# The decays' transfer issued by ScalarE, a planner constant for late transfers, and GpSimd's zeros ordered behind VectorE's clamp

## Chip, core and metric

The kernel runs on one core of one Trainium2 chip. The metric is the device time of one execution in microseconds; lower is better.

## What is computed

A linear attention with a decaying state, followed by a two-layer network with an exact GELU. All inputs are float32.

```python
batch, n_heads, seq, head_dim = (4, 8, 768, 48)
for t in range(S):
    kt, vt, rt = (k[:, :, t], v[:, :, t], r[:, :, t])
    cur = np.einsum('bhd,bhe->bhde', u[None] * kt, vt)
    y[:, :, t] = np.einsum('bhd,bhde->bhe', rt, state + cur)
    state = w[None, :, :, None] * state + np.einsum('bhd,bhe->bhde', kt, vt)
# x: y transposed to (3072 tokens, 384)
h = x @ w_in                                   # 384 -> 2048
g = 0.5 * h * (1.0 + erf(h * inv_sqrt2))
return g @ w_out                               # 2048 -> 384
```

`w` holds the decays (one for each head and channel), `u` the bonus of the current step.

## The kernel before

The sequence is cut into 6 chunks of 128 steps (`NCH`), the heads into 4 pairs (`NP`). Within a chunk the attention is done with matrix products. The powers of the decays scale r and k. The products of scaled k and r give the scores, and a mask and a diagonal are put in. The scores times v, plus the old state times r, give y. A group is one pair of heads in one chunk. The groups of the first chunk (`first_group`) have no old state and are the prologue: for each, VectorE multiplies r and k of the current step into `RK` (L559) and scales them by the powers into `Ts` (L553). TensorE sums `RK` times `u` (`sum_pairs`, L567), and ScalarE copies the sums to `cs` (L572). ScalarE or GpSimd puts the sums on the diagonal of `Am` (L580, L514). TensorE makes the scores (L586), VectorE copies them past the mask (L591), and TensorE multiplies by v (`new`, L605; `gaps`, L599, spreads the fourth pair over rows that are free). `keep` splits y into a high and a low part (`x3` and `xx`, L527 and L528), which are the network's input.

The network runs in float32 precision with three products of float32r parts (high and low weights `wh` and `wl`, high and low input). It has 16 steps of 128 hidden units for each chunk, 96 in all: `moe1` (L848, nine matmuls of 128x512 into the bank `Hp`), two GELUs on ScalarE (L880, L881), a subtraction on VectorE (L882) and `moe2` (L892, nine matmuls into `O`). During the first 16 steps the weights come in through three buffers `raw` (`w_load`, L482). They are taken apart by ScalarE (L497 into `wa`, L500 into `wb`, L506 into `wh`) and VectorE (L502, L509). The buffers `wa` must be zero beforehand (L439), as must be one half of `E` be ones (L466).

The decays and the bonus are one small tensor, `wu_sb` (112 partitions of 48 bytes). `clamp` (L418 to L421) sets ones in `W` and writes the clamped decays there. `powers` (L427, six multiplications) and `inverses` (L433, L434) make all powers from it, and ScalarE's `state_powers` (L446, L448) and three copies to `E` (L469) read them.

The order of the work is not the order of the program text. Each piece is handed to a `Plan` with an engine, a cost in nanoseconds, a due time and the names it reads and writes. `play` simulates the engines and picks, on each engine, the ready piece with the earliest due time. `run` repeats this for `ROUNDS` rounds and then tries `SEARCH` random changes of due times, drawn from `SEED`. It keeps what lowers `cost`, which is the end of TensorE's work in the plan plus the same end with every transfer `LATE` (600 ns) later. The best order is then issued. On the chip each engine takes its instructions strictly in that order and waits on semaphores where data demand it. Where TensorE has a hole in the plan during the prologue, `play` puts in `heat`, a matmul on zeros (L408).

For a transfer the plan keeps a common bus: it begins 1,050 ns after its issue, moves 412 bytes per ns, and lands 1,550 ns (600 for small ones) after its last byte. One more term is for transfers that were queued for over 1,200 ns:

```python
end = bus + (self.DMA_FIXED if ns > 20000 else self.DMA_SMALL)
end += self.DMA_SPREAD * (queued > self.DMA_QUEUED and bus > self.DMA_LATE)
```

`bus` is the time at which the transfer's last byte moves, `DMA_SPREAD` is 1,300 and `DMA_LATE` 16,000. All loads are issued by SyncE (SP), in the order of the plan. The first is `wu_sb` (L373), and then come the four tiles `T` of the prologue (L364), `N` (L367, L369) and the weights (L482). GpSimd's memsets have no semaphore on VectorE's work: the plan alone places `E` and the second `wa` after the clamp (they read the name `P0`, which the clamp writes), and on the chip they start as soon as GpSimd comes to them.

Of the kernel before, what the change touches and what calls it, by code (L numbers as in the profile page):

```python
# [18 lines left out]
ALU = mybir.AluOpType  # L19
# [12 lines left out]
HALF = 64  # L32
# [3 lines left out]
WMIN, WMAX = 0.7, 1.25  # L36
# [9 lines left out]
VISITS = (1, 6, 11)  # L46
POOL_DUE, POOL_CLASH, POOL_PE = 8000, 550, 2000
SWAP_DUE = 50000
ROUNDS, SEARCH, SEED, SPAN, LATE = 12, 2500, 5, (5000, 108000), 600
ROUND = "a"  # L50
LOADS = (1, 2, 3, "w0", "w1", 4, "u", "w2", 5)
AT_LOADS, AT_E = 14000, 15000
# [6 lines left out]
class Plan:  # L59
# [5 lines left out]
    OWN = {"act": 110, "dve": 110, "pool": 90}  # L65
    LAG = {"pe": 220, "act": 140, "dve": 115, "pool": 90, "sp": 0, "do": 0}
    DMA_GAP, DMA_LEAD, DMA_FIXED, DMA_SMALL, DMA_LANES = 480, 1050, 1550, 600, 8
    DMA_RATE, DMA_QUEUED, DMA_SPREAD, DMA_LATE = 412.0, 1200, 1300, 16000

    def __init__(self, after):  # L70
        self.after = after
# [3 lines left out]
    def add(self, eng, ns, at, fn, r=(), w=(), port=None):  # L75
        n = len(self.ops)
        deps = set()
        for x in r:
            deps.add(self.writer.get(x))
            self.readers.setdefault(x, []).append(n)  # L80
        for x in w:
            deps.add(self.writer.get(x))
            deps.update(self.readers.pop(x, ()))
            self.writer[x] = n
        deps -= {None, n}
        self.ops.append((eng, ns, at, fn, deps, eng == "pool" if port is None else port))
        self.reads.append(set(r))
        self.writes.append(set(w))
        return n

    def dma(self, nbytes, at, fn, r=(), w=(), gap=None):
        self.gaps[self.add("sp", nbytes, at, fn, r, w)] = gap or self.DMA_GAP
# [186 lines left out]
def rwkv_gelu_mlp(tc, rkT, rkv, wuT, uN, wmlp, r, k, vT, w, u, out):  # L279
    nc = tc.nc  # L280
    with ExitStack() as ctx:
# [7 lines left out]
        def sb(shape, dt, name, pool=None):  # L289
            return (pool or wk).tile(shape, dt, name=name)  # L290
# [8 lines left out]
        wu_sb = sb([LP, 3 * NP], F32, "wu_sb", cst)  # L299
        w_sb = wu_sb[:, 0:NP]  # L300
# [9 lines left out]
        W = sb([LP, NP, KEYS + C], F32, "W", pro)  # L310
        WKs = W[:, :, KEYS:]
        back = sb([LP, NP, 1], F32, "back", pro)
        E = sb([LP, NP, 2, 2, HALF], F32, "E")
# [16 lines left out]
        wa = [wa_all[:, i] for i in range(2)]  # L330
# [14 lines left out]
        def after(ins, one, reason="row tiles"):  # L345
            tc.add_manual_dep(ins.ins, one.ins.name, mybir.DependencyInfo(
                mybir.DependencyClass.Sync, mybir.DependencyReason.DATA), reason=reason)

        plan = Plan(after)
        add, dma = plan.add, plan.dma  # L350
        dve = lambda n: 65 + n / 0.96
        dve2 = lambda n: 65 + n / 1.92
        act = lambda n: 60 + n / 1.2
        pool = lambda n: 200 + n * 2.1
# [7 lines left out]
        def load_group(gi, at, r=()):  # L362
            s = slot(gi)
            dma(C * 4096, at, lambda: nc.sync.dma_start(T[s], rkT[gi]), r=[x for x in r if x[:8] != "free raw"], w=[f"T{s}"])  # L364
            if gi == 0:
                for i, x in ((1, "v"), (0, "k")):
                    dma(C * 1536, AT_LOADS + 800 * gi, lambda i=i: nc.sync.dma_start(N[s][:, i], rkv[gi, :, 1 + i]), r=r, w=[f"N{x}{s}"])  # L367
            elif gi < NP:
                dma(C * 3072, AT_LOADS + 800 * gi, lambda: nc.sync.dma_start(N[s], rkv[gi, :, 1:]), r=r, w=[f"Nk{s}", f"Nv{s}"])  # L369
            else:  # L370
                dma(C * 4608, at + 1, lambda: nc.sync.dma_start(N[s], rkv[gi]), r=[x for x in r if x != "free wb"], w=[f"Nr{s}", f"Nk{s}", f"Nv{s}"])

        dma(5000, -10 ** 6, lambda: nc.sync.dma_start(wu_sb, wuT), w=["w_sb"])  # L373
        load_group(0, LATER)


# [11 lines left out]
        for dst, src, x in ((diag2, diag, "diag"), (past2, past, "past")):  # L388
            for h in range(2):
                add("act", 245, LATER, lambda dst=dst, src=src, h=h: nc.scalar.copy(  # L390
                    out=dst[64 * h:64 * h + 64], in_=src[64 * h:64 * h + 64, 64 - 64 * h:128 - 64 * h]),
                    r=[x], w=[f"{x}2{h}"])
# [22 lines left out]
        plan.heat_from = add("pe", 430 * HEATS, 10, warm_up, r=["zeros"], w=["H", "A0", "A1", "O0", "O1", "O2", "Y", "U"])  # L415


        def clamp():  # L418
            nc.vector.memset(W[:, :, HALF:HALF + 1], 1.0)
            nc.vector.tensor_scalar(out=W[:, :, HALF + 1:HALF + 2], in0=w_sb.unsqueeze(2), scalar1=WMIN, scalar2=WMAX,  # L420
                                    op0=ALU.max, op1=ALU.min)  # L421

        def powers():
            n = 1
# [7 lines left out]
        def inverses():  # L432
            nc.vector.reciprocal(out=back, in_=W[:, :, C:C + 1])  # L433
            return nc.vector.tensor_tensor(out=W[:, :, 0:HALF], in0=W[:, :, HALF:C], in1=back.to_broadcast([LP, NP, HALF]),  # L434
                                           op=ALU.mult)

        add("dve", 170, -10 ** 6, clamp, r=["w_sb"], w=["P0"], port=True)
        for n, x in enumerate(wa):
            add("pool", 750, 5, lambda x=x: nc.gpsimd.memset(x, 0), r=["P0"] * n, w=["wa"], port=False)  # L439
        add("dve", 1380, 5, powers, r=["P0"], w=["P"], port=True)  # L440
        add("dve", 560, 6, inverses, r=["P"], w=["Wi"], port=True)

# [20 lines left out]
        add("act", 400, LATER, flipped(WN), r=["O0"], w=["WN"])  # L463


        add("pool", 520, 5, lambda: nc.gpsimd.memset(E[32:64, :, :, 1], 1.0), r=["P0"], w=["E0"], port=False)  # L466
        for i, (src, dst, h) in enumerate(((slice(0, LP), slice(0, LP), 0), (slice(0, D), slice(64, LP), 1),
                                           (slice(64, LP), slice(0, D), 1))):
            add("act", 630, AT_E, lambda src=src, dst=dst, h=h: nc.scalar.copy(  # L469
                out=E[dst].rearrange("l p a h i -> l (p a) h i")[:, :, h],  # L470
                in_=W[src].rearrange("l p (a i) -> l (p a) i", a=2)[:, :, 32:32 + HALF]),
                r=["Wi", "P", "WKs"], w=[f"E{(1, 2, 0)[i]}"], port=False)
        EVERY = [f"E{i}" for i in range(3)]
        for h in range(2):
            add("act", 480, LATER, lambda h=h: nc.scalar.copy(
                out=WN2[64 * h:64 * h + 64], in_=WN[0:64, :, ::1 - 2 * h]), r=["WN"], w=[f"WN2{h}"], port=False)
# [692 lines left out]
```

## Time and profile before

| | |
|---|---|
| median of 3 runs | 448.24 us (448.08 to 448.69) |
| profiled execution, its own time | 448.02 us |
| its span, first to last instruction | 446.3 us |
| mean granted TensorE clock | 0.998 |
| first 128x512 matmul of the network | 24.38 us after the span's start |
| last matmul ends | 441.8 us |

The span is what the rows below are counted in. The profiled execution took 1.72 us more than its span and 0.22 us less than the median of the runs. In the page and the rows PE is TensorE's matmuls, PEld its weight loads, DVE VectorE, ACT ScalarE, POOL GpSimd and SP SyncE. A q behind a name is the engine's sequencer, which issues transfers. Brackets at a row's end give the idle time just before it and what ended it. A tile's number is left out of its name, and L12 is line 12 of the kernel before.

### The profile page before, as it was taken

The page shows a single profiled execution, that of the slowest core. Times are in us where ns is not written, and L with a number is a line of the kernel's source. Part 1 is how long each engine was busy: PE and PEld are TensorE (multiplying, and loading weights), DVE is VectorE, ACT ScalarE, POOL GpSimd, SP SyncE. Part 2 cuts the span into 40 slices and gives each one's busy share as a digit, 9 for nine tenths or more (in the row PEclk, how much of TensorE's full clock was granted, in tenths as well). Part 3 has the DMA queues.
Part 4 walks back from the last instruction along what each step waited for, and adds up shares of the span by engine and source line. Part 5 has one row for each costly group of instructions (what it writes and reads, how often), then busy time and mean ns, then how long its engine had stood idle before and what let it go on. Part 6 is the DMA issues. An engine that isn't in the chain of part 4 may idle for free.

```text
span 446.3 us, 10492 instructions
## 1 busy us (share of the span) xinstructions
PE 439.0 (98%) x4626; PEld 380.1 (85%) x4626; DVE 230.2 (52%) x343; ACT 182.5 (41%) x321; POOL 72.0 (16%) x90
## 2 busy tenths in 40 slices
PE   8999999999999999999999999999999999999996
PEld 6788888888888888888888888888888888888885
DVE  7899999999541473513784433646233121211111
ACT  8989999522222223122233122223213232322221
POOL 2531113450220050002342001422000000000000
PEclk9999999999999999999999999999999999999999
DMA  8987798432600431006061004160100000100002
GB/s 298 390 294 250 244 310 269 149 120 75 214 1 0 131 96 71 1 1 210 12 218 71 3 0 160 54 218 8 72 1 2 13 10 17 71 1 0 0 1 76
DMA packets 13795, 46.15 MB, mean 103 GB/s; under 512 B 1904, under 2 KB 2544, under 8 KB 13744
## 3 DMA queue, kind: packets, MB, share of 16 engines
q1 hardware_dynamic: 13600, 45.29, 29.7%
q8 instruction: 38, 0.62, 0.6%
q14 instruction: 13, 0.11, 0.1%
q10 hardware_dynamic: 144, 0.13, 0.1%
HBM read 38.73 MB, written 4.72 MB: 97 GB/s over the span
## 4 chain that ended last, share of the span: by engine, by line
PE 80%; DVE 8%; ACT 4%; DMA 4%; issue 2%; SPq 1%; ACTq 0%; DVEq 0%
PE Hp L848 36%; PE O L892 35%; DMA raw<-in_wmlp_dram 4%; DVE wb L502 2%; PE Y L714 2%; PE A L727 2%; DVE wl L509 2%; PE Y L747 2%; DVE gl L882 2%; PE Y L892 1%; ACT wb L500 1%; ACT wa L497 1%; ACT wh L506 1%; PE Y L737 1%; DVE Am L788 1%
## 5 line engine op out<-in xcount | busy, mean ns | idle before, releaser
L848 PE MATMUL Hp<-xx,wh 128*128 128x512 f32 x570 | 155.8, 381 | 0.4 <-ACT gf L881 0.4
L882 DVE TENSOR_TENSOR gl<-gf,gh 128x512 fp32r<-128x512 f32 x92 | 67.2, 730 | 155.8 <-ACT gf L881 153.8
L880 ACT ACTIVATE gh<-Hp 128x512 fp32r<-128x512 f32 x91 | 54.5, 599 | 200.1 <-PE Hp L848 200.1
L848 PEld LDWEIGHTS Hp<-xx,wh 128*128 128x128 f32 x570 | 106.1, 189 | 16.4 <-ACT gf L881 1.2
L848 PE MATMUL Hp<-xx,wl 128*128 128x512 f32 x285 | 77.8, 380 | 0.1
L892 PE MATMUL O<-gl,wh 128*128 128x512 f32 (+1 forms) x276 | 74.2, 376 | 0.2 <-DVE gl L882 0.2
L892 PE MATMUL O<-gh,wl 128*128 128x512 f32 (+1 forms) x276 | 74.3, 376 | 0.0
L892 PE MATMUL O<-gh,wh 128*128 128x512 f32 (+1 forms) x276 | 73.9, 375 | 0.0
L848 PEld LDWEIGHTS Hp<-xx,wl 128*128 128x128 f32 x285 | 53.6, 189 | 7.9 <-DVE wl L509 0.3
L881 ACT ACTIVATE gf<-Hp 128x512 f32<-128x512 f32 x95 | 56.5, 595 | 6.8 <-PE Hp L848 4.5
L892 PEld LDWEIGHTS O<-gh,wh 128*128 128x128 f32 x276 | 52.1, 189 | 7.5 <-ACT gh L880 0.2
L892 PEld LDWEIGHTS O<-gl,wh 128*128 128x128 f32 x276 | 51.1, 189 | 7.6 <-DVE gl L882 0.6
L892 PEld LDWEIGHTS O<-gh,wl 128*128 128x128 f32 x276 | 51.0, 189 | 6.9
L719 POOL MEMSET done<- 1x1 f32 x13 | 1.1, 88 | 168.7 <-PE Y L714 168.3
L665 POOL TENSOR_TENSOR Nb<-Nb 128x384 f32<-128x384 f32 x12 | 12.1, 1008 | 55.0 <-DVE gl L882 37.8
L500 ACT ACTIVATE wb<-raw 128x768 int32<-128x768 uint32 x16 | 19.0, 1187 | 0.8 <-DMA raw<-in_wmlp_dram 0.8
L497 ACT ACTIVATE wa<-raw 128x768 f16<-128x768 bf16 x16 | 19.0, 1212 | 0.0
L671 POOL TENSOR_TENSOR Nb<-Nb,u_sb 128x384 f32<-128x384 f32 x12 | 12.1, 1005 | 33.2 <-DVE gl L882 28.3
L788 DVE COPY_PREDICATED Am<-past,A 128x512 f32<-128x512 uint32 x20 | 14.0, 736 | 6.6 <-PE A L727 6.4
L502 DVE CUSTOM_DVE_ANT_0 wb<-wb,wa 128x1536 uint16<-128x1536 uint16 x16 | 16.7, 1052 | 0.8 <-ACT wb L500 0.6
L662 DVE TENSOR_TENSOR Tb<-Tb,E 112x1024 f32<-112x1024 f32 x12 | 15.7, 1305 | 2.5 <-DMA Tb<-in_rkT_dram 2.5
L509 DVE TENSOR_TENSOR wl<-wb,wh 128x768 fp32r<-128x768 f32 x16 | 16.6, 1059 | 0.1
(172 smaller groups left out, 409.1 us busy)
## 6 DMA issues: line engine op xcount, KB each, us to landing
raw<-in_wmlp_dram SPq DMA_DIRECT2D x16, 767.8 KB, 6.2
Nb<-in_rkv_dram SPq DMA_DIRECT2D x12, 576.0 KB, 4.2
Tb<-in_rkT_dram SPq DMA_DIRECT2D x12, 512.0 KB, 7.4
raw<-in_rkv_dram SPq DMA_DIRECT2D x8, 576.0 KB, 5.2
wb<-in_rkT_dram SPq DMA_DIRECT2D x8, 512.0 KB, 7.5
out_dram<-raw SPq DMA_DIRECT2D x5, 512.0 KB, 2.8
T<-in_rkT_dram SPq DMA_DIRECT2D x4, 512.0 KB, 5.1
xx<-x SPq DMA_DIRECT2D x30, 64.0 KB, 6.0
```

The lines of the kernel that those rows point to most:

```text
L497: add("act", 930 if j < 2 else 1110, LATER, lambda: nc.scalar.activation(out=a.bitcast(F16).rearrange("p (n t) -> p n t", t=2)[:, :, 1], i ...
L500: add("act", 815 if j < 2 else 1110, LATER, lambda: nc.scalar.activation(out=b, in_=rest.bitcast(U32), func=AF.Copy, scale=2.0 ** -13), r= ...
L502: add("dve", dve(n), LATER, lambda: nc.vector.tensor_tensor(out=b, in0=b, in1=a, op=ALU.add), r=[A_], w=[B_], port=True)
L509: add("dve", dve(n), LATER, lambda: nc.vector.tensor_tensor(out=both(wl), in0=bf, in1=both(wh).bitcast(F32), op=ALU.subtract), r=[B_] + W_ ...
L662: add("dve", 1140, LATER, lambda: nc.vector.tensor_tensor(out=flat, in0=flat, in1=E[:, p, 0].rearrange("l h i -> l (h i)").unsqueeze(1).to ...
L665: add("pool", pool(DM), LATER, lambda: nc.gpsimd.tensor_tensor(out=n[:, 0], in0=n[:, 0], in1=n[:, 1], op=ALU.mult), r=[NK], w=[NR])
L788: add("dve", 625, LATER, lambda: nc.vector.copy_predicated(out=am, mask=past2.bitcast(U32).unsqueeze(1).unsqueeze(1).to_broadcast([C, 2, N ...
L848: nc.tensor.matmul(dst, lhsT=wt[j][:, 0, k_ * 128:(k_ + 1) * 128], rhs=pairs(x[:, a, k_, :]), start=start and k_ == ks[0], stop=stop and k ...
L880: add("act", 480, LATER, lambda: nc.scalar.activation(out=high, in_=dst, func=AF.Gelu, scale=256.0), r=[H_], w=[GH])
L881: add("act", 480, LATER, lambda: nc.scalar.activation(out=gf, in_=dst, func=AF.Gelu, scale=256.0), r=[H_], w=["gf"])
L882: add("dve", dve(512), LATER, lambda: nc.vector.tensor_tensor(out=low, in0=gf, in1=high.bitcast(F32), op=ALU.subtract), r=["gf", GH], w=[G ...
L892: nc.tensor.matmul(dst[:, a:b], lhsT=wt[j][:, 1, d * 128:(d + 1) * 128], rhs=pairs(gt)[:, a // 2:b // 2], start=(j == 0 and n == 0), stop= ...
```

## The change

ScalarE's queue issues the transfer of `wu_sb`, ahead of everything else on ScalarE. The plan holds 400 ns for the issue and 1,270 ns from there to the landing (an engine `do` that runs nothing). SyncE then begins with `T`. The two memsets of GpSimd that read `P0` in the plan (the second `wa` and `E`) get a real dependency on the clamp's last instruction, and the first `wa` has none as long as the plan issues it before the clamp. In the planner `DMA_LATE` becomes 12,000, so that the 1,300 ns also apply to queued transfers whose last byte moves between 12 and 16 us. The search has 1,500 tries instead of 2,500 and another seed, so any piece may come to stand elsewhere in its engine's order.

```diff
-ROUNDS, SEARCH, SEED, SPAN, LATE = 12, 2500, 5, (5000, 108000), 600
+ROUNDS, SEARCH, SEED, SPAN, LATE = 12, 1500, 2, (5000, 108000), 600
...
-    DMA_RATE, DMA_QUEUED, DMA_SPREAD, DMA_LATE = 412.0, 1200, 1300, 16000
+    DMA_RATE, DMA_QUEUED, DMA_SPREAD, DMA_LATE = 412.0, 1200, 1300, 12000
...
-        dma(5000, -10 ** 6, lambda: nc.sync.dma_start(wu_sb, wuT), w=["w_sb"])
+        add("act", 400, -2 * 10 ** 6, lambda: nc.scalar.dma_start(wu_sb, wuT), w=["w issue"])
+        add("do", 1270, -10 ** 6, lambda: None, r=["w issue"], w=["w_sb"])
...
+        clamped = []
+
+        def zero(x, value=0):
+            ins = nc.gpsimd.memset(x, value)
+            if clamped:
+                after(ins, clamped[0], "clamp")
+            return ins
+
         def clamp():
             nc.vector.memset(W[:, :, HALF:HALF + 1], 1.0)
-            nc.vector.tensor_scalar(out=W[:, :, HALF + 1:HALF + 2], in0=w_sb.unsqueeze(2), scalar1=WMIN, scalar2=WMAX,
-                                    op0=ALU.max, op1=ALU.min)
+            clamped.append(nc.vector.tensor_scalar(
+                out=W[:, :, HALF + 1:HALF + 2], in0=w_sb.unsqueeze(2), scalar1=WMIN, scalar2=WMAX, op0=ALU.max, op1=ALU.min))
+            return clamped[0]
...
-            add("pool", 750, 5, lambda x=x: nc.gpsimd.memset(x, 0), r=["P0"] * n, w=["wa"], port=False)
+            add("pool", 750, 5, lambda x=x: zero(x), r=["P0"] * n, w=["wa"], port=False)
...
-        add("pool", 520, 5, lambda: nc.gpsimd.memset(E[32:64, :, :, 1], 1.0), r=["P0"], w=["E0"], port=False)
+        add("pool", 520, 5, lambda: zero(E[32:64, :, :, 1], 1.0), r=["P0"], w=["E0"], port=False)
```

## Rows read from the trace of the kernel before

**Rows 1.** The page's first part: busy time, share, instructions of each engine.

```profile
PE 439.0 (98%) x4626; PEld 380.1 (85%) x4626; DVE 230.2 (52%) x343; ACT 182.5 (41%) x321; POOL 72.0 (16%) x90
```

**Rows 2.** Waits of PE, whole span: us in total, times, longest.

```profile
PE Y L586 <- ACT cs L572: 0.6, 1, 0.6
PE Hp L848 <- ACT gf L881: 0.4, 1, 0.4
PE O L892 <- DVE gl L882: 0.2, 1, 0.2
```

**Rows 3.** Busy time by stretch: PE, PEld, DVE, ACT, POOL; PEclk, DMA share, GB/s.

```profile
0.00:24.38 24.38, 22.25 (x319) 16.71 (x319) 20.16 (x32) 21.68 (x54) 9.24 (x17) 1.00 0.93 347
...
30.00:80.00 50.00, 49.56 (x643) 42.24 (x642) 48.55 (x67) 48.66 (x63) 12.24 (x15) 1.00 0.77 253
```

**Rows 4.** Timeline of PE, 15.5 to 20 us: start, length, instruction, idle before.

```profile
16.24 0.73 PE L408 MATMUL Hp<-zeros 128*128 128x512 f32 x2
17.54 1.16 PE L586 MATMUL Y<-Ts 64*128 64x128 f32 x16 [0.57 <-ACT cs L572]
```

**Rows 5.** Timeline of ACT, 14 to 18 us.

```profile
14.10 1.11 ACT L497 ACTIVATE wa<-raw 128x768 f16<-128x768 bf16 x1
16.03 0.92 ACT L500 ACTIVATE wb<-raw 128x768 int32<-128x768 uint32 x1 [0.83 <-DMA raw<-in_wmlp_dram]
16.85 0.57 ACT L527 CAST x<-O 112x512 fp32r<-112x512 f32 x1
17.32 0.17 ACT L572 COPY cs<-Y 128x8 f32<-128x8 f32 x1
```

**Rows 6.** Transfers issued at 1.28, 0.81 and 5.41 us: size, us to landing.

```profile
T<-in_rkT_dram SPq DMA_DIRECT2D x1, 512.0 KB, 3.9
wu_sb<-in_wuT_dram SPq DMA_DIRECT2D x1, 5.2 KB, 1.8
...
raw<-in_wmlp_dram SPq DMA_DIRECT2D x1, 767.8 KB, 10.6
```

**Rows 7.** Timeline of all engines, 0 to 14 us.

```profile
0.81 0.40 SPq L373 DMA_DIRECT2D wu_sb<-in_wuT_dram  x1
0.82 1.28 ACT L394 ACT_TABLE_LOAD   x1 [0.82 <-PEq L1156]
...
1.28 1.83 SPq L364 DMA_DIRECT2D T<-in_rkT_dram  x4
1.46 0.06 DVE L419 MEMSET W<- 112x4 f32 x1
...
2.58 0.52 POOL L466 MEMSET E<- 32x512 f32 x1
...
2.61 0.51 DVE L420 TENSOR_SCALAR W<-wu_sb 112x4 f32<-112x4 f32 x1 [1.09 <-DMA wu_sb<-in_wuT_dram]
...
3.15 0.74 POOL L439 MEMSET wa<- 128x768 int32 x1
3.16 1.41 DVE L427 TENSOR_TENSOR W<-W 112x4 f32<-112x4 f32 x6
...
4.59 0.30 ACT L448 COPY W<-W 112x128 f32<-112x128 f32 x1 [0.71 <-DVE W L427]
...
5.21 0.69 DVE L559 TENSOR_TENSOR RK<-T 112x512 f32<-112x512 f32 x1
...
6.61 0.60 ACT L469 COPY E<-W 112x512 f32<-112x512 f32 x1
```

**Rows 8.** Source line of SP's last stores: duration ns least, median, most; first, last start.

```profile
L936 SPq DMA_DIRECT2D out_dram<-raw x2: 333/354/374, 439.7 to 440.1; - x2
```

**Rows 9.** Timeline, 438.5 us to the end: ScalarE's only transfer.

```profile
440.31 0.39 ACTq L934 DMA_DIRECT2D out_dram<-raw  x1
```

**Rows 10.** DMA queues, 440.3 to 441.85 and 441.85 to 442.4 us: packets, MB, share.

```profile
q1 hardware_dynamic: 250, 0.48, 82.9%
...
q10 hardware_dynamic: 135, 0.12, 65.7%
```

## The prediction

> **What bounds the kernel now.** I begin with the page's busy times: TensorE's matmuls fill 98% of the span [rows 1]. So a change can gain only where TensorE has no useful work. The list of waits shows how little that is after the prologue: one hole of 0.4 us behind a GELU and one of 0.2 us behind VectorE's subtraction, and one of 0.6 us inside the prologue [rows 2]. The stretches show the rest: the network starts at 24.38 us, and of that prologue TensorE is busy 22.25 us, but partly with matmuls on zeros that fill holes [rows 3]. From there to the last matmul TensorE's work is fixed, so the end moves with the start of the network, less whatever later holes open. The timeline of TensorE shows where the prologue last loses time: two zero matmuls from 16.24 us, then 0.57 us of nothing, then the scores of the fourth group at 17.54 us, which waited for ScalarE's `cs` [rows 4]. From 17.54 us on TensorE goes without a hole into the network. The order on ScalarE tells why `cs` is late: it stands behind L500, which stood idle 0.83 us for a weight transfer [rows 5]. That transfer was issued at 5.41 us and landed 10.6 us later, at 16.0 us [rows 6].
>
> **The change, part by part.**
>
> *The issue of `wu_sb`.* SP issues it at 0.81 us in 0.40 us and comes to the first `T` at 1.28 us [rows 7]. Without it SP can issue `T` 0.47 us earlier. SP's transfers follow each other on a nearly full bus (DMA share 0.93 over the prologue [rows 3]), so each landing can come up to 0.47 us earlier; below, nothing at all. The first `T` lands 3.9 us after its issue, at 5.18 us [rows 6], and VectorE's first `RK` starts at 5.21 us [rows 7], just behind it. On ScalarE 0.40 us of issue come ahead of the table load; the cover is the idle 0.71 us before L448 at 4.59 us [rows 7], which would shrink to 0.31 us. If the powers also come 0.3 us earlier, that cover is just used up and nothing is lost. The landing of `wu_sb` itself was 1.8 us after the issue [rows 6]; I take the same from ScalarE's queue, from about 0.82 us, so 2.61 us again. A store from ScalarE's queue is the only row that may speak of this queue, and it is a rival below.
>
> How two sequencers issue at once the tail shows: SP's store took 333 ns alone and 374 ns beside ScalarE's of 386 ns [rows 8, 9], so overlap costs each some 0.05 us. The Trainium skill (Perfetto Trace Analysis, the section on HWDGE DMA instructions) says instead that the block that makes descriptors is locked for one instruction at a time. If the lock lasts the whole 0.40 us, `T` would be issued at 1.21 instead of 1.28 us and gain 0.07 us; no run here shows a full lock. That case is a rival.
>
> *The zeros behind the clamp.* The clamp took 0.51 us for 112x4 elements, from 2.61 to 3.12 us. `E`'s memset on GpSimd ran from 2.58 to 3.10 us [rows 7]: the clamp evidently ended when it did. Ones of the same shape took 0.06 us on VectorE, and a step of the powers beside the second `wa` memset took 1.41/6 = 0.235 us [rows 7]. These are the two bounds; the clamp is arithmetic like a power step, so I take 0.20 us and a gain of 0.31 us (bounds 0.28 and 0.45). The two memsets move to some 2.9 to 4.2 us, beside the powers. The six powers ran beside such a memset in the trace and show no stall like the clamp's, so I cost that at nothing; were they blocked, 0.52 + 0.74 = 1.26 us would be the price. Behind the waiting memsets on GpSimd stand the diagonals of the last two groups (L514), which wait for sums that are made much later. The memsets' readers start at 6.61 us (`E`) [rows 7] and 14.10 us (`wa`) [rows 5], so 2.4 us are to spare.
>
> Both parts together: the powers are ready 0.31 us earlier and `T` 0.47 us earlier, so VectorE's prologue starts 0.3 us earlier (bounds 0.07 and 0.45), and the bus with it. First term: **-0.3 us**.
>
> *The planner's constant.* The plan of before puts the last byte of the second weight tile at 13.15 us: 1.28 + 1.05, and 4.46 MB by the tile sizes of SP's first nine loads over 412 bytes per ns. That is under 16 us, so no 1.3 us is added, and the plan has it land at 14.7 us; it landed at 16.0 us [rows 6]. With 12 us as the border the 1.3 us are added and the plan's figure is right to within 0.1 us. It is an ordering number, not a time on the chip, but it says what will differ: L500 will no longer be put ahead of L527 and `cs` on ScalarE in the belief that its data are there. Then `cs` can come up to 0.83 us earlier [rows 5], the scores of the fourth group follow, and of the 1.30 us from 16.24 to 17.54 us something goes. Bounds: nothing (VectorE's mask copy or the next cast is late instead) and 1.30 us. I take the measured hole alone, 0.57 us [rows 4], because the zero matmuls stood where the plan already saw a hole with its early landing. Second term: **-0.57 us**.
>
> *The search.* Another seed and fewer tries reorder all pieces up to 108 us. The trace prices it only by what is there to win or lose: the 0.4 + 0.2 us of holes after the prologue [rows 2] can go, or come twice. I take zero, with 0.6 us either way.
>
> Sum: 448.02 - 0.3 - 0.57 = 447.15 us for an execution like the profiled one. That one lay 0.22 us below the median of the runs, so the forecast is 447.37, rounded to **447.4 us**.
>
> **The rivals.**
>
> *Given back between 30 and 80 us.* There ScalarE is busy 48.66 and VectorE 48.55 of 50 us [rows 3], on the splitting of the weights. If TensorE comes 0.9 us earlier and they don't, it waits for `wh` or `gl` by as much. For it: the holes of 0.4 and 0.2 us are behind these two engines. Against it: ScalarE and VectorE start their part of the prologue earlier too and have 2.7 and 4.2 us idle before 24.38 us. Only the sureness of a small shift would stay, 0 to 0.3 us: some 448.1 us.
>
> *`wu_sb` behind `T`, the slower side.* At the tail ScalarE's store was issued at 440.31 us [rows 9], yet up to 441.85 us only SP's queue moved data, 250 packets; in the next 0.55 us ScalarE's moved 135 [rows 10]. So a small transfer on ScalarE's queue may wait until SP's earlier ones have drained. If the first `T`, issued in the same moment, goes first, `wu_sb` lands with it at 0.81 + 3.9 = 4.71 us instead of 2.61. `RK` started 2.09 us after the clamp's end [rows 7], so it would start at 4.71 + 0.20 + 2.09 = 7.0 us, 1.8 us late. Less the 0.57 us that is 449.4 us; VectorE's later idle time can take up a part. It decides from a landing 0.9 us later than before, about 3.5 us, where both terms are spent, and at 4.4 us it is slower by 0.2%. Against it: the two were issued in sequence there, and here ScalarE can be first. The Trainium skill (DMA: Bandwidth & Descriptors, Queues, rings and completion order) says that an engine goes round between queues packet by packet. By it the decays would wait for one turn of `T` at most and this rival falls; the tail shows no such turn up to 441.85 us.
>
> *The full lock.* The descriptors of `wu_sb` and `T` are made one after the other whoever issues them. The first `T` then lands at 5.11 us, the first term shrinks to some 0.1 us, and the time is 447.6 us. The overlap of 374 and 386 ns speaks against it.
>
> *The new order wins more.* The whole 1.30 us and both later holes go with the 0.3: 448.24 - 2.2 = 446.0 at most, 446.5 taken.
>
> **Chances.** Forecast 0.42 (its own range 446.8 to 447.9), given back 0.20, `wu_sb` late 0.14, full lock 0.06, wins more 0.18. About 0.2%, 0.9 us, is what a measurement of this kernel can tell from no change; that border is 447.34 us. The forecast lies right at it: 0.24 of its 0.42 I give to faster and 0.18 to the same. With 0.18 from the larger win, faster is 0.42. Same is 0.18 + 0.20 + 0.06 and 0.02 of the late `wu_sb`: 0.46. Slower is the remaining 0.12. The range is 446.4 to 449.2 us: it holds the centres of all cases but the full price of a late `wu_sb`, and leaves out the best end of the larger win.
>
> **What would show it.** In the changed profile: the first `T` issued by SP near 0.81 us and landed near 4.7; the clamp starting at 2.6 and lasting 0.2 us or less; `RK` at 4.9 us; no idle time of ScalarE at L500 for the weights ahead of the fourth `cs`; the scores of the fourth group at some 16.7 us; the network's start near 23.5 us; and holes of TensorE after it of no more than 0.6 us. A clamp that starts after 3.5 us, a network that starts as late as 24.4 us, or new holes between 30 and 90 us would make it wrong.

## The result, and the profile after

The changed kernel takes 452.64 us (median of 5 runs, 450.54 to 453.28) against 448.26 us (448.08 to 448.69): the ratio is 1.0086, with a 95% interval of 1.0067 to 1.0105. It is slower by 4.4 us by the medians and by 3.9 us by the ratio. Medians here and below are over all runs; the ratios leave out a few runs of 571 to 1968 us in a slow state, and they are estimates of their own, not quotients of the medians (1.0098 here). The profiled execution took 452.9 us, with a span of 450.9 us.

TensorE's share on the page is 98% again, with 2.9 us more of busy time, and the waits name one hole that was not there [rows 1, 2]:

```profile
PE 441.9 (98%) x4625; PEld 383.3 (85%) x4625; DVE 230.2 (51%) x343; ACT 181.8 (40%) x321; POOL 71.5 (16%) x90
```

```profile
PE A L577 <- DVE RK L569: 1.8, 1, 1.8
...
PE O L902 <- DVE gl L892: 0.6, 1, 0.6
```

The timeline of the first 14 us tells where it comes from (the change moves the line numbers by up to 10; L429 is the clamp, L437 the powers, L569 `RK`):

```profile
0.81 1.81 SPq L364 DMA_DIRECT2D T<-in_rkT_dram  x4
0.81 0.41 ACTq L373 DMA_DIRECT2D wu_sb<-in_wuT_dram  x1
...
5.01 0.17 DVE L429 TENSOR_SCALAR W<-wu_sb 112x4 f32<-112x4 f32 x1 [3.48 <-DMA wu_sb<-in_wuT_dram]
...
5.22 1.41 DVE L437 TENSOR_TENSOR W<-W 112x4 f32<-112x4 f32 x6
5.24 0.74 POOL L422 MEMSET wa<- 128x768 int32 x1 [2.73 <-DVE W L429]
...
6.66 0.30 ACT L458 COPY W<-W 112x128 f32<-112x128 f32 x1 [2.35 <-DVE W L437]
...
7.22 0.68 DVE L569 TENSOR_TENSOR RK<-T 112x512 f32<-112x512 f32 x1
...
7.96 1.11 PE L577 MATMUL A<-wu_sb,RK 48*64 48x48 f32 x32 [1.76 <-DVE RK L569]
```

SP did come to `T` at 0.81 us, 0.47 us earlier, and the clamp without a neighbour takes 0.17 us instead of 0.51 [rows 7]. But the clamp starts at 5.01 instead of 2.61 us, and everything behind it is late: `RK` by 2.0 us, ScalarE's copy by 2.1 us. The landings of the two transfers issued at 0.81 us (size, us to landing) say why:

```profile
T<-in_rkT_dram SPq DMA_DIRECT2D x1, 512.0 KB, 4.0
wu_sb<-in_wuT_dram ACTq DMA_DIRECT2D x1, 5.2 KB, 4.2
```

The 5.2 KB of decays now need 4.2 us instead of 1.8 [rows 6], and land just behind the 512 KB of the first `T`. The DMA queues in four windows (1.5 to 2.3, 2.3 to 3.3, 3.3 to 4.3 and 4.3 to 5.1 us; packets, MB, share of 16 engines) show the order; q1 is SP's queue, q10 ScalarE's:

```profile
q1 hardware_dynamic: 14, 0.06, 38.1%
...
q1 hardware_dynamic: 52, 0.21, 85.9%
q10 hardware_dynamic: 34, 0.00, 2.2%
...
q1 hardware_dynamic: 108, 0.38, 95.0%
q10 hardware_dynamic: 92, 0.00, 6.0%
...
q1 hardware_dynamic: 85, 0.34, 102.1%
q10 hardware_dynamic: 2, 0.00, 0.2%
```

Up to 2.3 us only `T` moves; the first packets of the decays move at 2.6 us. From then on both queues move packets in nearly equal numbers, 92 of the decays' beside 108 of SP's in the third window, as if the DMA engines took them in turns. The decays are 5.2 KB in 128 packets, while SP's packets hold some 4 KB at first (0.06 MB in 14). So the small transfer takes as long as about as many large packets, and its last two move after 4.3 us. In the kernel before all 128 had moved between 1.8 and 2.3 us, ahead of `T`.

The late decays have a second effect, on TensorE's rate. Its timeline from 13 to 32 us, to be held beside [rows 4]:

```profile
13.96 2.07 PE L409 MATMUL Hp<-zeros 128*128 128x512 f32 x4
15.96 1.84 PE L596 MATMUL Y<-Ts 64*128 64x128 f32 x16
...
18.39 0.68 PE L577 MATMUL A<-wu_sb,RK 48*64 48x48 f32 x32
...
28.17 0.38 PE L858 MATMUL Hp<-xx,wh 128*128 128x512 f32 x1
```

The 16 scores take 1.84 us; before they took 1.16 us. A `sum_pairs` product takes 1.11 us at 7.96 us and 0.68 us at 18.39 us. Until some 17.5 us TensorE thus runs at the lower of its two levels, 1.2 instead of 2.4 GHz. In the kernel before such products were at full speed by 9 us:

```profile
8.10 1.16 PE L586 MATMUL A<-Ts 64*128 64x128 f32 x16
...
9.19 0.68 PE L567 MATMUL Y<-wu_sb,RK 48*64 48x48 f32 x32
```

(The clock column of the windows reads 1.00 from the start in both traces and can't show this; the durations do, and so do the starts: three zero matmuls from 3.43 us take 1.28 us to the start of the next, three matmuls of the network 0.65 us.) In front of the low stretch stands the hole: TensorE finished its ten zero matmuls at 6.2 us, still at the lower level, and then had nothing until 7.96 us. The network starts at 28.17 instead of 24.38 us, 3.8 us later. One product (L637 here, L627 before; 0.9 us) that came ahead of that start now comes behind it, at 28.91 us, so that the work is some 4.6 us late, as much as the span is longer.

### The profile page after: what moved, and what is told of

Same layout as the page of the kernel before. It is cut to its first block, busy times and chain, and to the rows that moved or that the text cites. A ratio compares the mean times of both kernels' runs of the same rounds, so it can differ in the third digit from the quotient of the medians.

```text
span 450.9 us, 10482 instructions
## 1 busy us (share of the span) xinstructions
PE 441.9 (98%) x4625; PEld 383.3 (85%) x4625; DVE 230.2 (51%) x343; ACT 181.8 (40%) x321; POOL 71.5 (16%) x90
## 4 chain that ended last, share of the span: by engine, by line
PE 85%; DVE 9%; issue 2%; ACT 1%; DMA 1%; POOL 0%; DVEq 0%; ACTq 0%
PE Hp L858 37%; PE O L902 35%; PE A L737 2%; PE Y L724 2%; DVE gl L892 2%; PE Y L757 2%; DVE wb L512 1%; PE Y L902 1%; DVE wl L519 1%; PE Hp L409 1%; DMA wu_sb<-in_wuT_dram 1%; PE O L615 1%; DVE Tb L672 1%; PE A L596 1%; PE Y L747 1%
## 5 line engine op out<-in xcount | busy, mean ns | idle before, releaser
L681 POOL TENSOR_TENSOR Nb<-Nb,u_sb 128x384 f32<-128x384 f32 x12 | 13.1, 1089 | 31.4 <-DVE gl L892 20.0
L512 DVE CUSTOM_DVE_ANT_0 wb<-wb,wa 128x1536 uint16<-128x1536 uint16 x16 | 16.7, 1048 | 0.1
```

The source lines that it names most:

```text
L512: add("dve", dve(n), LATER, lambda: nc.vector.tensor_tensor(out=b, in0=b, in1=a, op=ALU.add), r=[A_], w=[B_], port=True)
L681: add("pool", pool(DM), LATER, lambda: nc.gpsimd.tensor_tensor(out=n[:, 0], in0=n[:, 0], in1=u_sb[:, p, :].unsqueeze(1).to_broadcast([C, N ...
```

## The experiments

Times are medians beside runs of the kernel before on the same chip, in three groups, where that kernel took 448.20, 448.43 and 448.05 us. "The orders as they are" means that the planner still reckons with the old values, so that every engine's order is that of the kernel named.

**The decays from SP again, in the changed kernel's orders.**

```diff
-        add("act", 400, -2 * 10 ** 6, lambda: nc.scalar.dma_start(wu_sb, wuT), w=["w issue"])
+        add("act", 400, -2 * 10 ** 6, lambda: nc.sync.dma_start(wu_sb, wuT), w=["w issue"])
```

> The changed kernel with its orders as they are, but SyncE issues the decays' transfer, ahead of its first T, as before. Theory A (the loss is the late decays): the clamp starts near 2.6 us instead of 5.0, the powers start near 2.8, TensorE has no hole after its zero matmuls and its matmuls run at the full rate from about 7 us, not 17; the network starts some 3.5 to 4 us earlier than in the changed kernel and the time is 447.5 to 449. Theory B (the searched order is itself worse, the late decays cost only the 1.2 us net that the prediction gave them): the clamp is early all the same, but the time stays at 450.5 to 452.

448.23 us, ratio 1.0012 (0.9991 to 1.0032). All of the 4.4 us is gone. First the clamp on VectorE's timeline, then the network's start on TensorE's:

```profile
2.58 0.17 DVE L429 TENSOR_SCALAR W<-wu_sb 112x4 f32<-112x4 f32 x1 [1.06 <-DMA wu_sb<-in_wuT_dram]
```

```profile
22.82 0.38 PE L858 MATMUL Hp<-xx,wh 128*128 128x512 f32 x1
```

The network even starts 1.6 us earlier than before; 0.9 us of that is the product (L637) that now comes behind its start, so the lead is 0.7 us. The time gains nothing from it, though, and TensorE's waits and the timeline of VectorE and GpSimd from 95.5 to 98 us show where it went:

```profile
PE O L902 <- DVE gl L892: 1.2, 1, 1.2
```

```profile
96.06 0.99 POOL L678 TENSOR_TENSOR Nb<-Nb,WN 128x384 f32<-128x384 f32 x1
96.31 1.29 DVE L892 TENSOR_TENSOR gl<-gf,gh 128x512 fp32r<-128x512 f32 x1
```

The subtraction takes 1.29 us, where the median of the line's 92 is 693 ns. It starts while GpSimd's operation runs and ends at 97.60 us, 0.55 us behind that one's end. TensorE waits 1.2 us for it. So theory A holds (the loss is the late decays), and with the decays in time the rest of the change is worth nothing measurable.

**ScalarE issues, in the orders of the kernel before.**

```diff
-        dma(5000, -10 ** 6, lambda: nc.sync.dma_start(wu_sb, wuT), w=["w_sb"])
+        dma(5000, -10 ** 6, lambda: nc.scalar.dma_start(wu_sb, wuT), w=["w_sb"])
```

> The kernel before with its orders as they are, but ScalarE issues the decays' transfer. Theory A: the decays land behind the first T, at 4.7 to 5.1 us, RK starts 2 us late, TensorE is idle for over 1.5 us and its matmuls run at half rate for some 10 us more; the time is 450.5 to 453. Theory B: the decays are late too, but the time is 448.5 to 449.7.

452.41 us, ratio 1.0082 (1.0055 to 1.0108): this line alone, without the search, the constant or the zeros, costs what the whole change costs. The decays landed at 5.7 us, 4.9 us after their issue and again just behind the first `T`, and TensorE's longest wait is for `RK`, as in the changed kernel, and 0.7 us longer:

```profile
PE A L567 <- DVE RK L559: 2.5, 1, 2.5
```

**`T` held back.** In the changed kernel the first `T` waits for a memset of VectorE (`held[0]`, the one of `warm`) that ends at 0.94 us; the orders are as they are.

```diff
+            def tile():
+                ins = nc.sync.dma_start(T[s], rkT[gi])
+                if gi == 0:
+                    after(ins, held[0], "decays first")
+                return ins
...
```

> The changed kernel with SyncE's first T held behind VectorE's first memset, so that it is issued at about 1.0 us, some 0.2 us after the decays on ScalarE. Theory A in its form of a queue served in order of issue: the decays land near 2.6 us, T's landings are 0.2 to 0.3 us later than in the changed kernel and as much earlier than before; 447 to 448.5. Rival within A (ScalarE's queue is slow or takes turns with SyncE's, whoever issues first): the decays land at 3.5 us or later still, and the time stays over 449.5.

447.73 us, ratio 0.9988 (0.9968 to 1.0007). `T` was issued at 0.97 us, 0.16 us behind the decays, and the decays landed 2.2 us after their issue, at 3.0 us: far ahead of `T`, but 0.4 us behind the landing expected in theory A. A second kernel held `T` further, to 1.53 us (one run, 448.51 us):

> The changed kernel with SyncE's first T held until about 1.45 us, behind an additional memset of the zero tile on VectorE, some 0.6 us after ScalarE issues the decays. If only the order and distance of the two issues set the decays' landing, they land at 2.5 to 2.7 us, as from SyncE before. If ScalarE's queue is slower by itself, they land at 3.0 us again, as with T held to 0.97 us, though T's data now come later.

The landings of the decays, first with `T` at 0.97 us, then with `T` at 1.53 us:

```profile
wu_sb<-in_wuT_dram ACTq DMA_DIRECT2D x1, 5.2 KB, 2.2
```

```profile
wu_sb<-in_wuT_dram ACTq DMA_DIRECT2D x1, 5.2 KB, 1.7
```

With `T` 0, 0.16 and 0.7 us behind, the decays need 4.2, 2.2 and 1.7 us (4.1 to 4.9 us in the four kernels with a tie). The DMA queues tell why: with 0.16 us of lead 123 of the decays' 128 packets had moved by 2.1 us, beside 9 of `T`'s, and the last 5 came between 2.5 and 2.7 us; with 0.7 us of lead all 128 had moved by 2.3 us, before the first of `T`. ScalarE's queue is no slower than SP's, where it was 1.8 us [rows 6]; what counts is how many of the small packets move before the large ones begin. The rival of a slow queue falls. Its other half, that the queues take turns, doesn't: the packet counts of the tie look like turns.

**A longer row of zero matmuls.** The decays stay late; the hole in front of TensorE's first product is filled for the most part.

```diff
-            for n in range(HEATS):
+            for n in range(HEATS + 5):
```

> The changed kernel with 15 instead of 10 zero matmuls at the start, in the same plan, which bridge TensorE's hole from 6.2 to 8.0 us. The decays land as late as in the changed kernel. If TensorE's low rate up to 17 us follows from the hole, its matmuls run at the full rate from about 8 us, the network starts 2 to 2.7 us earlier than in the changed kernel and the time is 449.5 to 450.7. If the rate does not hang on the hole, or costs nothing because VectorE sets the pace, the time stays at 452 to 453.

450.01 us, ratio 1.0044 (1.0029 to 1.0059). By the medians that is 1.8 us slower than the kernel before and 2.6 us faster than the changed one (by the ratios 2.0 and 1.9 us). TensorE's timeline, to be held beside that of the changed kernel:

```profile
6.04 0.85 PE L409 MATMUL O<-zeros 128*128 128x512 f32 x3
6.73 0.40 PE L409 MATMUL A<-zeros 128*128 128x512 f32 x1
8.00 0.68 PE L577 MATMUL A<-wu_sb,RK 48*64 48x48 f32 x32 [0.87 <-DVE RK L569]
...
24.28 0.38 PE L858 MATMUL Hp<-xx,wh 128*128 128x512 f32 x1
```

The zero matmuls reach the full rate before they end; a hole of 0.87 us behind that does not end it, and the first product takes 0.68 instead of 1.11 us. The network starts 3.9 us earlier than in the changed kernel, where 2 to 2.7 us were expected. In this execution (451.05 us, the slowest of the five) TensorE's holes after that start come to 2.5 us, where the changed kernel had 0.6, and give part of it back. So 1.9 to 2.6 us hang on the longer row of zeros, and about as much stays.

What the added zeros do is less clear than expected. Here already the tenth one, at 5.57 us, takes 0.40 us, ahead of all that were added, while the tenth in the changed kernel takes 0.63 us. In the kernel of part one without the tie (below) the zeros run at the full rate from 4.67 us, and in the kernel before the product at 6.13 us still takes 1.11 us, all behind zeros that begin at 1.56 us. So the moment of the rise differs between executions, and no run tells apart whether the added zeros bring it or only shorten the hole behind it.

**The zeros alone**, on the kernel before (the diff of `zero` and `clamp` and nothing else):

> The kernel before with its orders as they are, and only the zeros of GpSimd behind VectorE's clamp. The clamp takes 0.17 us instead of 0.51 and the powers are ready 0.34 us earlier, but RK then waits for the first T at 5.2 us: VectorE's chain starts as before and the time is 447.7 to 448.7, no change. A rival, that ScalarE's earlier powers let the prologue end earlier, gives 447.9 or less with the network's start before 24.2 us.

448.36 us, ratio 1.0002 (0.9990 to 1.0015). The clamp took 0.17 us and `RK`, which stands behind the powers in VectorE's order, then waited for `T`:

```profile
2.45 0.17 DVE L428 TENSOR_SCALAR W<-wu_sb 112x4 f32<-112x4 f32 x1 [0.93 <-DMA wu_sb<-in_wuT_dram]
...
5.10 0.69 DVE L568 TENSOR_TENSOR RK<-T 112x512 f32<-112x512 f32 x1 [0.36 <-DMA T<-in_rkT_dram]
```

**Part one without the tie**, on the kernel before in its orders: ScalarE issues, `T` held to 0.97 us.

> The kernel before with its orders as they are, ScalarE issuing the decays and SyncE's first T held to 0.97 us: part one of the change alone, without the tie. The decays land at 3.0, T at 4.8 instead of 5.2 us. The clamp then ends at 3.2 and RK starts at 5.3 us, as before or 0.1 later: 447.9 to 448.7, so what the part could win is no more than 0.3 us. If the earlier stream of loads is worth something by itself, 447.6 or less.

447.88 us, ratio 0.9988 (0.9969 to 1.0007): `T` landed at 4.8, the decays at 3.0, `RK` started at 5.23 us.

**The planner told the truth**, twice. In the changed kernel 1,270 ns become 3,650; in the kernel with `T` held to 0.97 us they become 1,720. The plan then finds new orders.

> The changed kernel, whose plan is told that the decays land at 5 us (3,650 ns instead of 1,270), as they do. The decays stay late. The plan sees TensorE's hole, fills it with zero matmuls and orders the prologue for it: TensorE's full rate from about 7 us and 449 to 450.5. If what is lost is the late decays alone, whatever the plan knows, it stays at 451.5 to 453.

455.65 us, ratio 1.0160 (1.0139 to 1.0181): a miss, in an unexpected way. The first half came as expected: zero matmuls filled the prologue, it ran at full rate from 7.5 us, and the network started at 22.82 us with decays that landed at 4.9 us. But the new order opened holes later, 5.2 us in all after 24 us, the two longest of 1.66 us at 104.8 and 1.67 us at 152.6 us. The holes do not make up all of the 7.2 us lost; the rest stays open.

```profile
104.82 0.69 PE L737 MATMUL A<-Tb 48*64 48x64 f32 x32 [1.66 <-DVE wa L791]
```

> The changed kernel with T held to 0.97 us as in the run with the tile behind the decays, and a plan that is told the decays land at 3.06 us (1,720 ns). An attempt at a better kernel than both: the orders fit what happens, 447 to 448. A new order may as well put holes between 60 and 100 us: up to 449.

448.80 us, ratio 1.0012 (1.0002 to 1.0022): no better than the same kernel with the orders that it had.

**The constant alone**, on the kernel before:

> The kernel before with the planner's border at 12 instead of 16 us, and nothing else. If the prediction's second step is right, ScalarE no longer idles 0.8 us at L500 ahead of the fourth group's sums and the network starts before 24 us; theory A says that such a lead is given back in holes of TensorE between 60 and 100 us, so that the time is 447.6 to 448.8, no change. If the lead is kept, 447.5 or less.

451.36 us, ratio 1.0056 (1.0034 to 1.0078): slower, which no theory had. The prologue did in part what the prediction said: ScalarE's idle time at L500 is gone and the network starts at 21.89 us. But 1.9 of the 2.5 us of lead are two products (L605, L627) that now come behind that start, and the scores of the fourth group come at 18.56 us, later than before. The runs fall into two groups, four of 449.3 to 449.7 us and eight of 450.9 to 452.6 us, and the profile is of one of the eight (451.97 us). Its timelines of GpSimd, VectorE and TensorE, one after the other, and two windows (the column behind POOL's is the granted clock) show the price there:

```profile
67.87 6.99 POOL L668 TENSOR_TENSOR Nb<-Nb,WN 128x384 f32<-128x384 f32 x1
74.81 0.09 POOL L719 MEMSET done<- 1x1 f32 x1
```

```profile
67.84 0.95 DVE L502 CUSTOM_DVE_ANT_0 wb<-wb,wa 128x1536 uint16<-128x1536 uint16 x1
...
72.18 1.83 DVE L502 CUSTOM_DVE_ANT_0 wb<-wb,wa 128x1536 uint16<-128x1536 uint16 x2
75.79 0.41 DVE L781 SCALAR_TENSOR_TENSOR Sb<-Sa,E,A 48x192 f32<-48x192 f32 x1 [1.78 <-PE A L737]
```

```profile
74.92 0.82 PE L737 MATMUL A<-Nb 64*48 64x48 f32 x32 [1.95 <-POOL done L719]
```

```profile
60.00:75.00 15.00, 12.79 (x122) 10.41 (x124) 13.82 (x20) 13.88 (x18) 8.14 (x4) 1.00 0.81 287
75.10:78.40 3.30, 3.30 (x69) 2.79 (x62) 2.37 (x4) 1.75 (x3) 0.75 (x1) 0.50 0.41 122
```

A multiplication on GpSimd that takes 1.0 us elsewhere takes 6.99 us. It starts with VectorE's operation at 67.84 us and ends only 0.85 us after the last of a chain of VectorE operations without a gap (67.84 to 74.01 us). TensorE's next product waits for GpSimd's `done` behind it, and after that hole of 1.95 us the granted clock is 0.50 from 75.1 to 78.4 us. The Trainium skill (SBUF — State Buffer, Who interferes with whom) says that a VectorE operation with two inputs in SBUF and a GpSimd operation that reads SBUF lock each other out for a whole instruction. The trace agrees and goes further: over a gapless run of such operations GpSimd didn't get its turn at all. That this lock is the cause was read from the trace; no run took it away. Nor does a trace show what the four faster runs did.

**The search alone**, on the kernel before:

> The kernel before with 1,500 tries and the other seed, and nothing else. The decays come from SyncE at 2.6 us. Theory A: an order among many, 447.5 to 449. Theory B (the search is what makes the changed kernel slow): 450 or more.

448.44 us, ratio 1.0007 (0.9990 to 1.0023). Theory B falls: the seed and the number of tries, by themselves, cost nothing measurable. The network starts at 23.50 us here, with no product moved behind it: a lead of 0.9 us, no smaller than with the constant, and none of it is left at the end.

## Why the prediction was wrong, point by point

*The landing of `wu_sb` is the step that failed.* The prediction took "the same from ScalarE's queue", 2.61 us, and gave the opposite 0.14. The rows to decide by were in hand: ScalarE's only store had moved nothing beside SP's up to 441.85 us [rows 10]. I set against them that ScalarE could be first. It was not: both were issued at 0.81 us, and `T`'s data moved first. The decays landed at 4.99 us, 2.4 us later than taken. The rival's landing, 4.71 us, was close, and so was `RK`'s start, 7.0 against 7.22 us, but in part by luck. The rival let the decays wait until `T` had drained; in the trace they move beside it, packet for packet from 2.6 us on, and land just behind it, probably because `T` too has some 128 packets (512 KB in packets of 4 KB).

*The rival's price was mis-sized*: 449.4 us forecast, 452.6 measured. Two things were missing. The first is TensorE's rate: the rival counted VectorE's delay and did not ask what TensorE does in the meantime. Its ten zero matmuls ended at 6.2 us, and a longer row of them saves 1.9 to 2.6 us. The second is the 0.57 us of the constant, which the rival took off and which the time did not keep.

*The lock and the turns.* The full lock of the Trainium skill (Perfetto Trace Analysis, the section on HWDGE DMA instructions) did not show in the issues: those of 0.81 us ran side by side, in 0.39 and 0.41 us. But the decays' first packets moved 1.8 us after their issue, against 1.0 us with `T` held back; what kept them, no run tells. The turns between queues, packet by packet, that the Trainium skill states (DMA: Bandwidth & Descriptors, Queues, rings and completion order), fit the trace, with 92 packets beside 108. What failed is the conclusion from them, that the decays wait for one turn of `T` at most. They are 128 packets on 16 engines, eight each if spread evenly (an estimate), and each of these can wait for a turn. They landed 0.18 us behind all of `T`.

*The first term* (-0.3 us) could not be told from nothing. Without the tie, part one gave 0.9988 (0.9969 to 1.0007), which holds both 0 and -0.3 us. The prediction took both parts as early at once. In the runs one of the two stayed late: `RK` needs `T` and stands behind the powers, and it started at 5.1 to 5.2 us, held by the tile with the zeros alone, and by the powers with ScalarE's issue, where the decays landed at 3.0 and not at 2.6 us.

*The zeros* did on VectorE what was forecast: 0.17 us for the clamp against the 0.20 taken, and powers beside a memset in the same 1.41 us. In the two kernels without that dependency in which the clamp ran beside the longer memset of `wa` (constant alone, search alone), it took 0.81 and 0.82 us. Alone the zeros had no measurable effect on the time.

*The second term* (-0.57 us) was right in part as a mechanism and wrong as a gain. With the constant, ScalarE's wait at L500 and the hole ahead of the fourth group's scores are gone, but those scores come at 18.0 (decays from SP again) and 18.6 us (constant alone) and not at the 16.7 us forecast. The network starts 1.6 and 2.5 us earlier, of which 0.7 and 0.6 us are a lead and the rest is moved work. The size is thus close to the term, but the search alone gave 0.9 us without the constant. The orders pay it back in holes behind 60 us, 1.2 us in the one case and, with the constant alone, more than had been gained. The prediction had this as the rival "given back", but laid it to a lack of work capacity on ScalarE and VectorE. In both traces the holes stand behind an operation of VectorE or GpSimd that ran long beside the other engine; that the two lock each other out is the likely cause, not a shown one.

*The search* was costed at zero with 0.6 us either way. Alone it was zero within the interval; but five orders of the same work, all with the decays by 3.1 us, ran from 447.7 to 451.4 us, so the bounds for a new order were too narrow.

No version beat the kernel before by more than its measurement is uncertain. The nearest are the two with `T` held to 0.97 us, at a ratio of 0.9988 each.

## What to carry to other kernels

A small load on which everything waits has to be issued ahead of the large ones by a clear distance, whichever engine issues it: giving it another queue is no priority, and a tie here cost 2.4 us of landing. Count its packets and not its bytes: 128 packets of a few bytes went beside as many of some 4 KB. When something early gets late, ask what the engines behind it do meanwhile; here a hole of TensorE in its warm-up cost its length and was followed by a stretch at half rate. And a planner's gain at the start of a plan counts only when the end moves, above all where its model of a shared resource is coarse.

## What was not expected of the hardware

The landing of 5.2 KB depended on its distance to a 512 KB transfer on another queue: 4.2 us in a tie, 2.2 us with 0.16 us of lead, 1.7 us with 0.7 us. Beside a large transfer its packets moved about one for one with the other queue's. A GpSimd multiplication of 1.0 us took 6.99 us beside VectorE's gapless run. The same ten zero matmuls from 1.56 us brought TensorE to its full rate at 4.67 us in one execution and after 6.2 us in others. TensorE ran at its lower level for some 10 us after a hole of 1.76 us that came before it had reached the full rate, although it then had work again; a hole of 0.87 us at 7.1 us, with the full rate reached, left it there. Whether the length of the hole or its place decides, no run tells apart.
